# The tail of a decode block: a diagonal product moved forward, first-layer products interleaved, and the output stored after a block transpose on VectorE

## The chip, the cores and the metric

The kernel runs on one core of one Trainium2 chip. The metric is the device time of one execution in microseconds (us). The kernel before takes 667.69 us (median of 3 runs, 667.66 to 667.77). Nine executions of this kernel in one set of rounds lay between 667.60 and 667.92 us, so one kernel spreads by up to about 0.3 us, and its median moved from 667.69 to 667.81 us between sets of rounds.

Engine names as in the profile: PE is the matrix engine and PEld its weight loads, DVE is VectorE, ACT is ScalarE (the Activation engine), POOL is GpSimd, SP is the engine that issues DMAs. ACTq and SPq are the DMA issues of ACT and SP. A DMA has "landed" when the last increment of its completion semaphore has come. P.V is the product of the softmax weights with the values, oT its result for one quad (explained below), and yo the kernel's result before it is transposed and stored.

## The reference, cut to what matters

```python
x = A_x                                            # (4, 1, 512)
mod = (_silu(c) @ w_mod)...                        # six modulation vectors sa, ca, ga, sb, cb, gb
h = _layernorm(x) * (1 + ca) + sa
x = x + ga * attention(h, k_cache, v_cache, wq, wo)   # 4 batches, 32 heads, 4096 keys of 128: 268 MB of cache
h = _layernorm(x) * (1 + cb) + sb
z = gelu(h @ w_in)                                 # w_in: 512 x 1792
z1, z2 = z[..., :896], layernorm(z[..., 896:])
y = (z1 * (z2 * w_sp + b_sp)) @ w_out              # the sequence length is 1: w_sp and b_sp are scalars
return x + gb * y                                  # (4, 1, 512), bf16
```

The key and value caches stream through the core once. Everything else is small, but the last weights (wo, w_in, w_out) arrive at the end of the stream, and the feed-forward part can only follow them.

## The kernel before

The work goes over 32 "quads" (four heads of one batch element). The last quad (31) takes its P.V product in another form than the others, with v as weights, because v comes in five pieces:

```python
def values_last(i, n0, n1):
    P4 = P4s[i % NB]
    if n0 == 0:
        zsum(i)
    for n in range(n0, n1):
        nc.tensor.matmul(st["o", i], lhsT=st["v", i][:, n, :], rhs=P4[:, n, :], ...)
...
values_last(NQ - 1, 0, 3 * NT // 4)
diagonal(NQ - 2)                 # f32 products (four calls, eight in the trace) that take quad 30's result out of its block form
project(NQ - 2)                  # divide by the softmax sum into oT
values_last(NQ - 1, 3 * NT // 4, NT)
project(NQ - 1)                  # oT of quad 31, then the product with the last wo
```

After the attention, the first layer is 56 products from two w_in tiles (a=0: three quarters of the rows, a=1: the last quarter, loaded after it), first for z2 (s=1), then for z1 (s=0):

```python
for s in (1, 0):
    for a, (a0, a1) in enumerate(WJS):             # WJS = [(0, 3), (3, 4)]
        ...                                        # 21 products for a=0, 7 for a=1
            nc.tensor.matmul(zp[s][:, jf], lhsT=win[a][:, j - a0, cols], rhs=h[:, j], ...)
```

The result yo has the model dimension over the partitions. It is transposed on PE, copied from PSUM by DVE, and stored by one DMA of 16 rows of 256 bytes:

```python
nc.vector.tensor_tensor(out=yo.rearrange("p b j -> p j b"), in0=q, in1=r1, op=ALU.add)
t_ps = psum_s.tile([J * B, P], F32, name="small", bufs=1)
nc.tensor.matmul(t_ps, lhsT=yo.rearrange("p b j -> p (b j)"), rhs=ident, start=True, stop=True)
ot = post.tile([J * B, P], BF16, name="ot")
nc.vector.tensor_copy(out=ot, in_=t_ps)
nc.sync.dma_start(out=out.rearrange("b s (j p) -> (b s j) p", p=P), in_=ot)
```

## Time and profile before

| | before |
|---|---|
| time | 667.69 us |
| span of the profile | 666.0 us |
| mean rate of the loads | 425 GB/s |
| last wo lands, projection starts | 654.54, 654.58 us |
| yo ends | 662.89 us |
| store issued, landed | 663.60, 664.97 us |

The page of the profile first: its length, the mean busy share of the DMA engines in 40 slices (in tenths), and the first line of the chain that ended last.

```profile
span 666.0 us, 6938 instructions
...
DMA  9999999999999999999999999999999999999995
...
DMA 58%; PE 26%; DVE 14%; ACT 1%; issue 1%; SPq 0%; DVEq 0%; ACTq 0%
```

The loads are busy everywhere except in the last slice. The change touches the last 20 us only, so most of the time cannot move. The chain of waits from 630 us on (start, length, what):

```profile
631.71 22.83 DMA wo_g<-in_A_wo_dram
...
654.58 0.60 PE attn_ps L401 x16
...
658.24 0.77 PE z_ps L491 x21
...
659.05 1.25 PE z_ps L491 x35
...
660.56 1.28 ACT L506
...
663.26 0.28 DVE ot L535
```

The projection waits for the load of the last wo; then follow the statistics, the z products, the load of the activation table at 660.56, and the output. The timeline shows the instructions that the change moves (start, length, engine and line, operation, in brackets the idle time before and what ended it):

```profile
651.57 1.85 PE L354 MATMUL zo_ps<-sel,osb 128*128 128x4 f32 x8
...
653.28 0.99 PE L364 MATMUL zo_ps<-P_1_109,vt 128*128 128x4 bf16 x32
...
654.31 0.17 DVE L376 TENSOR_TENSOR oT<-zo_ps,rz 128x4 bf16<-128x4 f32 x1 [0.38 <-PE zo_ps L364]
654.58 0.51 PEld L401 LDWEIGHTS <-wo_g 128*128 128x128 bf16 x16 [0.39 <-DMA wo_g<-in_A_wo_dram]
...
658.21 0.72 PEld L491 LDWEIGHTS <-win_434 128*128 128x128 bf16 x21 [1.86 <-DMA win_434<-in_B_w_in_dram]
...
659.04 0.29 PEld L491 LDWEIGHTS <-win_435 128*128 128x128 bf16 x7
...
659.26 0.72 PEld L491 LDWEIGHTS <-win_434 128*128 128x128 bf16 x21
...
660.32 0.22 ACT L502 ACTIVATE u<-z_ps 128x56 bf16<-128x56 f32 x1 [0.67 <-PE z_ps L491]
...
662.70 0.20 DVE L529 TENSOR_TENSOR yo<-q,r_4229 128x16 bf16<-128x16 f32 x1
...
662.95 0.28 PE L531 MATMUL small<-ident,yo 128*16 128x128 bf16 x1 [1.24 <-DVE yo L529]
663.26 0.28 DVE L535 CAST ot<-small 16x128 bf16<-16x128 f32 x1 [0.37 <-PE small L531]
663.60 0.36 SPq L536 DMA_DIRECT2D out_dram<-ot  x1
```

Three things are to be seen. The diagonal stands at 651.57, between two pieces of the last P.V. The projection at 654.58 had a DMA as its last releaser, not oT. From the end of yo to the issue of the store 0.71 us pass.

Last, what SP waited for in the same view, from 662 us on:

```profile
SPq L562 <- DMA out_dram<-ot: 0.8, 1, 0.8
```

That is the end of the program: SP waits for the store to land.

### The profile page before, as it was taken

The numbers are of one execution on the slowest core, as the hardware profiler recorded it, in microseconds if no ns is written. First come the engines' busy times: TensorE is split into PE (matmuls) and PEld (weight loads), VectorE is DVE, ScalarE is ACT, GpSimd is POOL, SyncE is SP. The second block draws the span as 40 slices with busy tenths as digits, with TensorE's granted clock in tenths as the row PEclk, the third lists the DMA queues.
The fourth block names the chain that finished last, engine by engine and source line by source line (L and its number), as shares of the span: only waits on it lengthen the run. The fifth ranks groups of instructions, "written<-read, shape, count | busy, mean of one in ns | idle before, by whom it ended". The sixth has DMA issues, their size and how long they took to land.

```text
span 666.0 us, 6938 instructions
## 1 busy us (share of the span) xinstructions
PE 413.0 (62%) x3024; PEld 203.9 (31%) x3024; DVE 402.8 (60%) x475; ACT 41.3 (6%) x115; POOL 4.7 (1%) x21
## 2 busy tenths in 40 slices
PE   2567777646577664576655577655566656557765
PEld 2223333322233322232222333222223322223335
DVE  2166677665556575547576456757555757655762
ACT  1200000000000000000000000000000000000002
POOL 2000000000000000000000000000000000000000
PEclk9977777768887677887676787766788757788895
DMA  9999999999999999999999999999999999999995
GB/s 378 432 428 431 434 433 430 432 435 430 431 434 435 430 428 436 435 426 432 439 433 422 434 441 430 423 437 439 428 433 429 439 429 434 429 436 431 430 415 226
DMA packets 12733, 283.17 MB, mean 425 GB/s; under 512 B 1432, under 2 KB 1952, under 8 KB 4000
## 3 DMA queue, kind: packets, MB, share of 16 engines
q1 hardware_dynamic: 12624, 282.73, 98.8%
q8 instruction: 23, 0.38, 0.2%
q14 instruction: 6, 0.05, 0.0%
q0 software_dynamic: 64, 0.00, 0.0%
q10 hardware_dynamic: 16, 0.01, 0.0%
HBM read 282.73 MB, written 0.00 MB: 425 GB/s over the span
## 4 chain that ended last, share of the span: by engine, by line
DMA 58%; PE 26%; DVE 14%; ACT 1%; issue 1%; SPq 0%; DVEq 0%; ACTq 0%
DMA kt<-in_A_k_cache_dram 55%; PE s_ps L281 25%; DVE kt L276 12%; DMA wo_g<-in_A_wo_dram 3%; DVE S L290 0%; SPq L92 0%; PE z_ps L491 0%; PE big L341 0%; ACT E L311 0%; DVE P_0_105 L314 0%; ACT L506 0%; DVE nm L308 0%; DVE mT L300 0%; DVE hm L302 0%; DVE hb L304 0%
## 5 line engine op out<-in xcount | busy, mean ns | idle before, releaser
L281 PE MATMUL s_ps<-kt,ident 128*128 128x512 bf16 x1024 | 291.9, 455 | 188.1 <-DVE kt L276 188.1
L276 DVE TENSOR_TENSOR kt<-kt,qbc 128x8192 bf16<-128x8192 bf16 x64 | 282.7, 4420 | 84.2 <-DMA kt<-in_A_k_cache_dram 84.1
L281 PEld LDWEIGHTS <-ident 128*128 128x128 bf16 x1024 | 115.8, 113 | 352.9 <-issue 228.3
L290 DVE TENSOR_REDUCE S<-s_ps 128x64 f32<-128x512 f32 x64 | 44.3, 692 | 123.9 <-PE s_ps L281 123.9
L354 PE MATMUL zo_ps<-sel,osb 128*128 128x4 f32 x248 | 33.9, 260 | 25.8 <-ACT osb L347 25.8
L311 ACT ACTIVATE E<-S,nm 128x128 f32<-128x128 f32 x32 | 12.8, 402 | 566.1 <-DVE nm L308 566.1
L354 PEld LDWEIGHTS zo_ps<-sel,osb 128*128 128x128 f32 x248 | 31.4, 198 | 37.2 <-ACT osb L347 37.2
L341 PE MATMUL big<-vt,P_0_105 128*32 128x512 bf16 x352 | 21.0, 380 | 1.5 <-DMA vt<-in_A_v_cache_dram 1.5
L341 PE MATMUL big<-vt,P_1_109 128*32 128x512 bf16 x320 | 19.1, 380 | 0.0
L341 PE MATMUL big<-vt,P_2_113 128*32 128x512 bf16 x320 | 19.1, 380 | 0.0
L347 ACT COPY osb<-big 128x512 f32<-128x512 f32 x31 | 17.6, 566 | 18.3 <-PE big L341 18.3
L314 DVE TENSOR_TENSOR P_1_109<-E,mask_99 128x512 bf16<-128x512 f32 x11 | 7.6, 693 | 6.8 <-ACT E L311 6.8
L314 DVE TENSOR_TENSOR P_0_105<-E,mask_99 128x512 bf16<-128x512 f32 x11 | 7.6, 693 | 6.7 <-ACT E L311 6.7
L215 PE MATMUL big<-vt,hbc 128*32 128x512 bf16 x128 | 8.6, 434 | 5.0 <-DMA vt<-in_A_wq_dram 5.0
L341 PEld LDWEIGHTS <-P_0_105 128*32 128x32 bf16 x352 | 8.4, 96 | 8.9 <-DMA vt<-in_A_v_cache_dram 1.6
L314 DVE TENSOR_TENSOR P_2_113<-E,mask_99 128x512 bf16<-128x512 f32 x10 | 6.9, 692 | 6.2 <-ACT E L311 6.2
L375 DVE RECIPROCAL rz<-zo_ps 128x4 f32<-128x4 f32 x31 | 5.5, 176 | 8.2 <-PE zo_ps L354 8.2
L401 PE MATMUL attn_ps<-oP,wo_g 128*128 128x4 bf16 x112 | 3.8, 164 | 10.6 <-DVE oP L398 10.6
L341 PEld LDWEIGHTS <-P_2_113 128*32 128x32 bf16 x320 | 7.6, 96 | 6.7
L341 PEld LDWEIGHTS <-P_1_109 128*32 128x32 bf16 x320 | 7.6, 96 | 6.7
L401 PEld LDWEIGHTS <-wo_g 128*128 128x128 bf16 x128 | 4.3, 97 | 10.9 <-issue 10.4
L308 DVE STREAM_TRANSPOSE nm<-hb 128x32 f32<-128x32 f32 x32 | 6.8, 212 | 1.1
(218 smaller groups left out, 130.3 us busy)
## 6 DMA issues: line engine op xcount, KB each, us to landing
kt<-in_A_k_cache_dram SPq DMA_DIRECT2D x31, 4096.0 KB, 25.7
vt<-in_A_v_cache_dram SPq DMA_DIRECT2D x31, 4096.0 KB, 33.7
vt<-in_A_wq_dram SPq DMA_DIRECT2D x1, 4096.0 KB, 20.5
wo_g<-in_A_wo_dram SPq DMA_DIRECT2D x8, 512.0 KB, 26.6
kt<-in_A_k_cache_dram SPq DMA_DIRECT2D x2, 2048.0 KB, 24.1
vt<-in_w_mod_dram SPq DMA_DIRECT2D x1, 3072.0 KB, 10.0
vt<-in_A_v_cache_dram SPq DMA_DIRECT2D x1, 2048.0 KB, 18.8
win_434<-in_B_w_in_dram SPq DMA_DIRECT2D x1, 1344.0 KB, 24.3
```

Of the source, the lines that this page charges most:

```text
L215: nc.tensor.matmul(qp[hl * R:(hl + 1) * R, 0:n], lhsT=hbc[:, j, b, :], rhs=wv[:, g0:g0 + n, hl, :], start=(j == 0), stop=(j == J - 1), til ...
L276: nc.vector.tensor_tensor(out=kt, in0=kt, in1=q[:, None, :].to_broadcast([P, HT, DH]), op=ALU.mult,)
L281: nc.tensor.matmul(ps, lhsT=ident, rhs=kt[:, :, cc * DC:(cc + 1) * DC], start=(cc == 0), stop=(cc == DH // DC - 1),)
L290: nc.vector.tensor_reduce(out=st["S", i][:, half * HT:(half + 1) * HT], in_=st.pop(("s", i, half)), axis=AX.X, op=ALU.add,)
L308: nc.vector.transpose(out=nm, in_=hb)
L311: nc.scalar.activation(out=E, in_=S, func=AF.Exp, bias=nm[:, 0:1], scale=att_scale, accum_out=rs,)
L314: nc.vector.tensor_tensor(out=P4[:, 0:NT, :], in0=E[:, :, None].to_broadcast([P, NT, NH]), in1=mask4[:, None, :].to_broadcast([P, NT, NH]) ...
L341: nc.tensor.matmul(po[32 * t:32 * t + 32], lhsT=P4[:, n0:n0 + 8, :], rhs=st["v", i][:, n0:n0 + 4, :], start=(u == 0), stop=(u == NU - 1), ...
L347: nc.scalar.copy(out=osb, in_=po)
L354: nc.tensor.matmul(st["o", i], lhsT=osb[:, n, :], rhs=sel[:, NH * n:NH * n + NH], start=(n == 0), stop=(n == 3),)
L375: nc.vector.reciprocal(out=rz, in_=st.pop(("z", i)))
L401: nc.tensor.matmul(attn_ps[:, jo, :], lhsT=wo_g[:, hl, jo * P:(jo + 1) * P], rhs=oT[:, hl, :], start=(g == 0 and hl == 0 and jo == 0), sto ...
```

## The change

The intent: move the diagonal of quad 30 into time in which PE waits for v, so that the last P.V is not held up; give PE nine z1 products to do where z2 would wait for the second w_in tile; and shorten the output by transposing 32x32 blocks on DVE, straight into SBUF. The block transpose puts 16 useful rows at the head of each 32 partitions, so four stores are needed, two on SP and two on ACT. The core of the diff:

```diff
-        values_last(NQ - 1, 0, 3 * NT // 4)
         diagonal(NQ - 2)
         project(NQ - 2)
-        values_last(NQ - 1, 3 * NT // 4, NT)
+        values_last(NQ - 1)
         project(NQ - 1)
 ...
+        yo = post.tile([P, 2, B, J], BF16, name="yo")
+        nc.gpsimd.memset(yo, 0.0)
 ...
-        for s in (1, 0):
-            for a, (a0, a1) in enumerate(WJS):
-            ...                                   # products in the order of the loops
+        z0a = zmm[0, 0]
+        for s, jf, a, j in zmm[1, 0] + z0a[:9] + zmm[1, 1] + z0a[9:] + zmm[0, 1]:
+            ...                                   # the same 56 products
 ...
-        t_ps = psum_s.tile([J * B, P], F32, name="small", bufs=1)
-        nc.tensor.matmul(
-            t_ps, lhsT=yo.rearrange("p b j -> p (b j)"), rhs=ident, start=True, stop=True,
-        )
-        ot = post.tile([J * B, P], BF16, name="ot")
-        nc.vector.tensor_copy(out=ot, in_=t_ps)
-        nc.sync.dma_start(out=out.rearrange("b s (j p) -> (b s j) p", p=P), in_=ot)
+        ot = post.tile([P, R], BF16, name="ot")
+        nc.vector.transpose(out=ot, in_=yo.rearrange("p t b j -> p (t b j)"))
+        ov = out.rearrange("b s (j k r) -> k (b s j) r", j=J, r=R)
+        for k in range(P // R):
+            eng = nc.sync if k % 2 == 0 else nc.scalar
+            eng.dma_start(out=ov[k], in_=ot[k * R:k * R + B * J])
```

I call the three pieces part 1 (diagonal), part 2 (z1 products) and part 3 (output).

More of the change, by code (lines that the diff above doesn't have):

```diff
@@ L357, in diagonal, with values_last @@
                 )
-        def values_last(i, n0, n1):
+        def values_last(i):
             P4 = P4s[i % NB]
-            if n0 == 0:
-                zsum(i)
-            for n in range(n0, n1):
+            zsum(i)
+            for n in range(NT):
                 nc.tensor.matmul(
@@ L483 @@
         zp = {s: psum.tile([P, JF, B], F32, name=f"z{s}_ps") for s in (1, 0)}
+        zmm = {}
         for s in (1, 0):
             for a, (a0, a1) in enumerate(WJS):
-                for j0, j1 in JFS:
-                    for jf in range(j0, j1):
-                        c0 = s * FH + j0 * P + jf - j0
-                        cols = slice(c0, c0 + (P - 1) * (j1 - j0) + 1, j1 - j0)
-                        for j in range(a0, a1):
-                            nc.tensor.matmul(
-                                zp[s][:, jf], lhsT=win[a][:, j - a0, cols], rhs=h[:, j],
-                                start=(j == 0 and jf == 0), stop=(j == J - 1),
-                                skip_group_check=True,
-                            )
+                zmm[s, a] = [
+                    (s, jf, a, j) for jf in range(JF) for j in range(a0, a1)
+                ]
+        z0a = zmm[0, 0]
+        for s, jf, a, j in zmm[1, 0] + z0a[:9] + zmm[1, 1] + z0a[9:] + zmm[0, 1]:
+            j0, j1 = JFS[jf >= JFS[0][1]]
+            c0 = s * FH + j0 * P + jf - j0
+            nc.tensor.matmul(
+                zp[s][:, jf],
+                lhsT=win[a][:, j - WJS[a][0], c0:c0 + (P - 1) * (j1 - j0) + 1:j1 - j0],
+                rhs=h[:, j], start=(j == 0 and jf == 0), stop=(j == J - 1),
+                skip_group_check=True,
+            )
         z2b = post.tile([P, 2, JF, B], F32, name="z2b")
@@ L527 @@
         nc.vector.tensor_tensor(out=q, in0=q, in1=bc(rstd, J), op=ALU.mult)
-        yo = post.tile([P, B, J], BF16, name="yo")
-        nc.vector.tensor_tensor(out=yo.rearrange("p b j -> p j b"), in0=q, in1=r1, op=ALU.add)
-        t_ps = psum_s.tile([J * B, P], F32, name="small", bufs=1)
-        nc.tensor.matmul(
-            t_ps, lhsT=yo.rearrange("p b j -> p (b j)"), rhs=ident, start=True, stop=True,
-        )
-        ot = post.tile([J * B, P], BF16, name="ot")
-        nc.vector.tensor_copy(out=ot, in_=t_ps)
-        nc.sync.dma_start(out=out.rearrange("b s (j p) -> (b s j) p", p=P), in_=ot)
+        nc.vector.tensor_tensor(
+            out=yo[:, 0].rearrange("p b j -> p j b"), in0=q, in1=r1, op=ALU.add,
+        )
+        ot = post.tile([P, R], BF16, name="ot")
[4 more added lines that the diff above has]
+            eng.dma_start(out=ov[k], in_=ot[k * R:k * R + B * J])
 _INS = ['A_x', 'A_k_cache', 'A_v_cache', 'A_wq', 'A_wo', 'B_x', 'B_w_in', 'B_w_sp', 'B_b_sp', 'B_w_out', 'c', 'w_mod']
```

## The prediction

> **What bounds the kernel now.** The page shows the DMA engines at 9 tenths or more in 39 of 40 slices, 425 GB/s over a span of 666.0 us. The change touches only what comes after 645 us, so almost none of the 667.69 us can move. In the chain of waits the tail runs: load of the last wo_g lands at 654.54 -> projection 654.58 -> h ends 658.09 -> z products 658.24 to 660.28 -> gelu u 660.32-660.54 -> table load to 661.84 -> Ln, Exp to 662.39 -> q -> yo ends 662.90 -> PE transpose to 663.24 -> cast to 663.54 -> store issued 663.60, landing 1.4 us later -> end 666.0.
>
> **Part 1, diagonal 30 and project(30) ahead of the last P.V.** The timeline shows the eight f32 products (1.85 us) at 651.57-653.42 between the P.V pieces. PE is idle 645.7-648.27 and osb is copied by 646.01, so they move into idle time. The last P.V can then follow the last v piece (landing about 653.1), and the last oT end near 653.7 instead of 654.48. But the projection then waits for wo_g, landing at 654.54: before it began at 654.58, with a DMA as the last releaser. Gain at most 0.1 us, estimated 0.03.
>
> **Part 2, z1 products where z2 waits for w_in.** This trace has no such wait: the z2 products of the first w_in tile end at 659.02, those of the second start at 659.05. All 56 products remain, so gelu u still comes at about 660.3. The nine products put first (about 37 ns each) delay gelu z2 by about 0.33 us, from 659.46 to about 659.8, still ahead of gelu u. The z2 statistics product moves from 660.14 to about 660.26, y's start from 660.81 by at most 0.1, mostly hidden by the table load, which bounds rstd. Effect 0 to +0.1 us.
>
> **Part 3, output.** Removed after yo: a PE product (0.28), a cast from PSUM (0.28) and hops, 0.64 us in all. Added: one DVE block transpose; the kernel's own 128x32 ones take 0.21 us, so ot is ready about 0.24 us after yo: 0.40 us earlier. (The Trainium skill, "VectorE: DVE Perf Modes", The three transpose paths: on VectorE only 32x32 blocks, into SBUF. Hence four stores.) But each queue now issues two stores. SP issues take 0.33-0.43 us here, the out store 0.36; the Activation queue's two at the start took 0.56 and 0.26. The second issue thus starts about 0.35-0.6 us after the first, near 663.6-663.8, like the old single store. The Trainium skill ("DMA: Bandwidth & Descriptors", Issuing engines are not separate DMA queues) says a second issuer saves only issue time. Sum: -0.1 to +0.2 us.
>
> **Sum.** Part 1 -0.03, part 2 +0.02, part 3 -0.1 (estimates): 667.58 us, range 667.1 to 668.1. Chances: faster by over 2% 0.01, within 2% 0.98, slower 0.01.
>
> **What would show it.** Diagonal 30 at about 646-648 and the last oT before 654, yet the projection still released by wo_g near 654.5. Gelu z2 near 659.8, gelu u within 0.1 of 660.3 after the same landing. The DVE transpose 0.2 us, the first store issued about 0.3 us after yo (was 0.70), the second about 0.4 after that, landing 1.4 us after its issue.
>
> **What would make it wrong.** wo_g landing earlier than the trace suggests (then part 1 pays up to 0.7 us); stores of 64 bytes landing slower than those of 256; a slow first issue on the Activation queue; w_in landing later (then part 2 pays up to 0.3 us).

## More of the kernel before

Weight loads that do not wait overlap in this trace: the 7 of win_435 begin at 659.04 and take 0.29, yet the next group begins at 659.26. But the first group ends at 658.93 and win_435 begins only at 659.04. There is a gap of 0.11 us, which no bracket reports.

## The result, and the profile after

The changed kernel takes 668.17 us (median of 6 runs, 668.05 to 668.27), the kernel before 667.72 us in the same rounds (6 runs, 667.66 to 667.93). Ratios are the mean time of one kernel's runs over that of the other's of the same rounds, so not quite the ratio of the medians: 1.0006 with an interval of 0.9993 to 1.0019. By that interval the two are the same. In microseconds the two sets of six runs do not overlap, and by their medians the change costs 0.45 us. The prediction said 667.58 us with a range of 667.1 to 668.1. The measured time lies 0.07 us above the range, and the sign of the small difference was wrong.

The same views of the changed kernel. The page:

```profile
span 666.2 us, 6941 instructions
...
DMA  9999999999999999999999999999999999999995
...
DMA 61%; PE 24%; DVE 12%; ACT 1%; issue 0%; SPq 0%; DVEq 0%
```

The chain of waits:

```profile
632.45 22.09 DMA wo_g<-in_A_wo_dram
...
654.58 0.60 PE attn_ps L400 x16
...
658.24 1.87 PE z_ps L494 x56
...
660.37 1.28 ACT L510
...
662.74 0.21 DVE ot L537
```

The timeline:

```profile
646.07 1.06 PE L354 MATMUL zo_ps<-sel,osb 128*128 128x4 f32 x8 [0.75 <-ACT osb L347]
...
653.68 0.17 DVE L375 TENSOR_TENSOR oT<-zo_ps,rz 128x4 bf16<-128x4 f32 x1 [6.05 <-PE zo_ps L363]
654.57 0.51 PEld L400 LDWEIGHTS <-wo_g 128*128 128x128 bf16 x16 [1.02 <-DMA wo_g<-in_A_wo_dram]
...
658.21 1.02 PEld L494 LDWEIGHTS <-win_434 128*128 128x128 bf16 x30 [1.86 <-DMA win_434<-in_B_w_in_dram]
...
659.15 0.30 PEld L494 LDWEIGHTS <-win_435 128*128 128x128 bf16 x7
...
660.13 0.22 ACT L506 ACTIVATE u<-z_ps 128x56 bf16<-128x56 f32 x1 [0.37 <-PE z_ps L494]
...
662.51 0.20 DVE L533 TENSOR_TENSOR yo<-q,r_4231 128x16 bf16<-128x16 f32 x1
662.74 0.21 DVE L537 STREAM_TRANSPOSE ot<-yo 128x32 bf16<-128x32 bf16 x1
662.99 0.85 ACTq L541 DMA_DIRECT2D out_dram<-ot  x2
663.02 0.83 SPq L541 DMA_DIRECT2D out_dram<-ot  x2
```

And SP's wait at the end:

```profile
SPq L567 <- DMA out_dram<-ot: 1.1, 1, 1.1
```

The diagonal moved into idle time and the last oT comes 0.63 us earlier (653.68 for 654.31), but the projection starts at the same 654.58, released by wo_g. The 56 z products are one unbroken run (the win_435 group begins before the end of the group ahead of it), and gelu u comes 0.19 us earlier at 660.13 for 660.32. The transposed output is ready 0.59 us earlier. And still the span is longer. The chain now ends at 662.95, and what follows is not in it.

To see the end, I read from the trace when each store's semaphore increments came and what SP did afterwards. SP ends the program by waiting for the semaphores that the program's DMAs and engines use, one or two in each wait, one wait after the other. "Landed" is the last of a store's 16 increments; SP's "closing drain" is its first instruction after all these waits that signals the other engines. Times in us from the start of the span:

| | before | after | difference |
|---|---|---|---|
| projection starts | 654.58 | 654.58 | -0.01 |
| yo ends | 662.89 | 662.71 | -0.19 |
| last store issued | 663.60 | 663.43 | -0.18 |
| last store landed | 664.97 | 664.98 | +0.01 |
| SP's closing drain | 665.23 | 665.42 | +0.18 |
| span | 665.98 | 666.17 | +0.19 |
| time of this run | 667.75 | 668.05 | +0.30 |

So in these two executions 0.19 us were gained before the output, 0.20 lost up to the last landing, 0.17 lost between the landing and SP's drain, and 0.11 lost outside the span. The profiled execution of the changed kernel is the fastest of its six, which is why its difference is 0.30 and that of the medians 0.45. (Differences are taken before rounding.) The waits of SP, as the trace has them (start and length; before, the store's semaphore is the fourth waited for, after, the last store's is the second):

```
before   664.016 0.028   wait 1
         664.080 0.028   wait 2
         664.142 0.028   wait 3
         664.990 0.028   wait 4: the store (landed 664.974)
         665.052 0.028   wait 5
         665.111 0.028   wait 6
         665.179 0.007   wait 7
         665.234 0.007   closing drain
after    663.902 0.017   wait 1
         663.955 1.051   wait 2: the last store (landed 664.984)
         665.046 0.028   wait 3
         665.110 0.028   wait 4
         665.172 0.028   wait 5: first store on ACT (landed 664.351)
         665.231 0.028   wait 6: first store on SP (landed 664.518)
         665.293 0.028   wait 7: second store on ACT (landed 664.821)
         665.358 0.007   wait 8
         665.416 0.007   closing drain
```

A wait whose semaphore is long complete still costs about 0.06 us. Those ahead of the landing are free; those behind it are not.

### The profile page after: what moved, and what is told of

It is laid out like the page before. It is cut to its first block, busy times and chain, and to the rows that moved or that the text cites. A ratio compares the mean times of both kernels' runs of the same rounds, so it can differ in the third digit from the quotient of the medians.

```text
span 666.2 us, 6941 instructions
## 1 busy us (share of the span) xinstructions
PE 414.6 (62%) x3022; PEld 203.6 (31%) x3023; DVE 402.8 (60%) x475; ACT 41.3 (6%) x115; POOL 4.8 (1%) x22
## 4 chain that ended last, share of the span: by engine, by line
DMA 61%; PE 24%; DVE 12%; ACT 1%; issue 0%; SPq 0%; DVEq 0%
DMA kt<-in_A_k_cache_dram 58%; PE s_ps L281 24%; DVE kt L276 11%; DMA wo_g<-in_A_wo_dram 3%; SPq L92 0%; PE z_ps L494 0%; PE big L341 0%; DVE S L290 0%; ACT L510 0%; ACT E L311 0%; DVE P_1_109 L314 0%; DVE P_0_105 L314 0%; PE small L155 0%; PE attn_ps L400 0%; DVE mT L300 0%
## 5 line engine op out<-in xcount | busy, mean ns | idle before, releaser
L354 PEld LDWEIGHTS zo_ps<-sel,osb 128*128 128x128 f32 x248 | 30.0, 191 | 38.4 <-ACT osb L347 38.4
L375 DVE TENSOR_TENSOR oT<-zo_ps,rz 128x4 bf16<-128x4 f32 x32 | 5.4, 169 | 7.1 <-PE zo_ps L363 6.0
```

The costliest lines, as they stand in the source:

```text
L354: nc.tensor.matmul(st["o", i], lhsT=osb[:, n, :], rhs=sel[:, NH * n:NH * n + NH], start=(n == 0), stop=(n == 3),)
L375: nc.vector.tensor_tensor(out=oT[:, :, b], in0=st.pop(("o", i)), in1=rz, op=ALU.mult,)
```

## The experiments

My theory: parts 1 and 2 gain a little; part 3 loses it and more, (a) because the second store of each queue is issued 0.4 us after the first, (b) because two stores issued at once complete one after the other, (c) because the last store's semaphore is among the first that SP waits for, and (d) by something after the span. Rivals: the reordering of PE hurts; stores of 64-byte rows are slow by themselves; the second queue is slow. "Against before" compares medians of the same rounds.

### Part 1 alone

```diff
-        values_last(NQ - 1, 0, 3 * NT // 4)
         diagonal(NQ - 2)
         project(NQ - 2)
-        values_last(NQ - 1, 3 * NT // 4, NT)
+        values_last(NQ - 1)
```

> Part 1 alone (diagonal 30 and project(30) ahead of the last P.V; z order and output as before). Both theories: the last oT ends near 653.8 us but the projection still starts at 654.58 us because wo_g lands then, so the time equals the kernel before within 0.08 us. If part 1 were the cause of the loss, +0.3 us or more.

Measured: 667.68 us (667.53 to 667.88) against 667.81 us (667.60 to 667.92), -0.13 us, a little more than the 0.08 that I allowed and with ranges that overlap. The projection started at 654.58 us, 0.05 after wo_g landed at 654.53. Part 1 is not the loss.

### Parts 1 and 2, with the old output

Taken from the changed kernel, with the output of before put back:

```diff
-        yo = post.tile([P, 2, B, J], BF16, name="yo")
-        nc.gpsimd.memset(yo, 0.0)
 ...
-        ot = post.tile([P, R], BF16, name="ot")
-        ...                                # block transpose, four stores
+        ...                                # PE transpose, copy, one store, as before
```

> Parts 1 and 2 with the old output (PE transpose, cast, one store of 16 rows of 256 bytes). My theory: the changed z order removes a hidden wait of about 0.17 us for the second w_in tile, so 0.15 to 0.22 us faster than before, and the whole loss sits in the output. Rival (the reordering hurts): slower than before by 0.2 us or more.

Measured: 667.67 us (667.58 to 667.70) against 667.81, -0.14 us: at the edge of what I expected, and the rival fails. In the total it cannot be told from part 1 alone, because wo_g happened to land 0.10 us later in this profile (654.63). From the first z product to the end of yo it takes 4.47 us, as in the changed kernel (4.47); the three runs with the old z order took 4.65 (before), 4.57 (part 1 alone) and 4.54 (part 3 alone, below). So part 2 is worth 0.07 to 0.18 us, and its worth depends on how long after h the second w_in tile lands. The z products themselves show it without exception: from the first start to the last they take 1.69 us here and in the changed kernel, 1.88, 1.80 and 1.77 us in the three with the old order. (In three later runs with part 2, yo came 4.52 to 4.63 us after the first z product although the z products took no longer; in the run with the unused tile the trace shows y waiting for the last w_out tile.) In the kernel before, the second w_in tile landed at 659.00 and the first product with it started at 659.05, 0.195 us after the one ahead of it; with part 2 no two z products start more than 0.05 us apart.

### Part 3 alone

```diff
+        yo = post.tile([P, 2, B, J], BF16, name="yo")
+        nc.gpsimd.memset(yo, 0.0)
 ...
-        ...                                # PE transpose, copy, one store
+        ...                                # block transpose, four stores, as in the change
```

> Part 3 alone on the kernel before. My theory: the last store lands about 0.2 us later after yo than the old one, SP then has about 0.18 us more of semaphore checks, and something after the span adds about 0.1: +0.45 to +0.7 us against before. Rival (the loss comes from parts 1 and 2): within 0.15 us of before.

Measured: 668.28 us (668.12 to 668.44) against 667.81, +0.47 us. The whole loss is in part 3. The last store landed 2.28 us after yo (before: 2.08), SP's drain came 0.43 us after the landing (before: 0.26), and 1.95 us of the profiled time lay outside the span (before: 1.77): 0.20 + 0.17 + 0.18 us. Part 1's absence shows too: here the projection started at 654.64, released by oT, 0.13 us after wo_g landed, so part 1 is worth up to 0.08 us in some executions.

```profile
654.64 0.57 PE L401 MATMUL attn_ps<-oT,wo_g 128*128 128x4 bf16 x16 [0.26 <-DVE oT L376]
```

### The order of the last waits

The loads of c and x are cut, which changes which semaphore each later DMA uses. The last store's semaphore is then waited for fifth of the eight (I had written "fourth of seven"; what matters is what follows it).

```diff
-    nc.scalar.dma_start(out=rows[0:B], in_=c)
-    nc.scalar.dma_start(out=rows[B:2 * B], in_=A_x.rearrange("b s d -> (b s) d"))
+    xr = A_x.rearrange("b s d -> (b s) d")
+    for src, r0, cuts in ((c, 0, [0, 1, 2, 3, 4]), (xr, B, [0, 1, 2, 4])):
+        for a, b in zip(cuts[:-1], cuts[1:]):
+            nc.scalar.dma_start(out=rows[r0 + a:r0 + b], in_=src[a:b])
```

> The changed kernel with the loads of c and x at the start cut into 7 instead of 2, which moves every later DMA by five completion semaphores, so that the last store's semaphore is the fourth of the seven that SP checks at the end, as the old store's was, not the second. My theory: 0.10 to 0.15 us faster than the changed kernel (about +0.3 us against before instead of +0.45). Rival (the number or the size of the stores alone costs the time): the same as the changed kernel, +0.45 us against before.

Measured: 667.85 us (667.81 to 668.02) against 667.81, +0.04 us, so about 0.4 us better than the changed kernel was in its own rounds, more than I expected. The wait did what the theory says: from the last landing to the drain 0.261 us, as before, instead of 0.432. The step outside the span is gone as well (1.77 us instead of 1.88), which I had not counted on. These make 0.17 + 0.11 = 0.28 us. The rest is mostly the yardstick: the kernel before measured 667.81 us in these rounds and 667.72 us in those of the changed kernel, and without it the two medians (667.85, 668.17) differ by 0.32 us. Cutting loads at the start also moves the start of the stream, so this kernel is not a clean change of one thing.

### One store, two stores, four stores on one queue

These ask what a store costs. The first two store only a quarter and a half of the output. Their outputs are wrong, which doesn't matter for the times.

```diff
-        for k in range(P // R):
+        for k in range(1):
```

> The changed kernel with only the first of its four stores (16 rows of 64 bytes, on SP), so three quarters of the output are wrong on purpose. My theory (rows of 64 bytes cost nothing, the count of stores does): the store lands about 1.37 us after its issue, as the 256-byte rows did, so about 1.68 us after yo instead of 2.07 to 2.08, and the time is about 0.5 us below the kernel before. Rival (64-byte rows land slower): landing 1.5 us or more after the issue.

```diff
-        for k in range(P // R):
+        for k in range(2):
```

> The changed kernel with the first two of its four stores, one on each queue, so half of the output is wrong on purpose. My theory: both are issued at once, but their completions come one after the other, so the later lands about 1.50 us after its issue, 0.13 later than in one_block; time within 0.0 to 0.2 us of one_block. Rival (the two queues are independent): both land about 1.37 us after their issue.

```diff
-            eng = nc.sync if k % 2 == 0 else nc.scalar
+            eng = nc.sync
```

> The changed kernel with all four stores on the SP queue. My theory: each further issue costs about 0.42 us on the queue, so the last is issued about 1.25 us after the first and lands about 0.7 us later than in the changed kernel: +1.0 to +1.3 us against before. Rival (completions, not issues, set the pace, or the second queue is what hurts): at or below the changed kernel's +0.45 us.

The issues in the three timelines, first one block, then two, then four on SP:

```profile
662.67 0.21 DVE L537 STREAM_TRANSPOSE ot<-yo 128x32 bf16<-128x32 bf16 x1
662.94 0.36 SPq L541 DMA_DIRECT2D out_dram<-ot  x1
```

```profile
662.48 0.21 DVE L537 STREAM_TRANSPOSE ot<-yo 128x32 bf16<-128x32 bf16 x1
662.73 0.38 ACTq L541 DMA_DIRECT2D out_dram<-ot  x1
662.76 0.36 SPq L541 DMA_DIRECT2D out_dram<-ot  x1
```

```profile
662.80 0.21 DVE L537 STREAM_TRANSPOSE ot<-yo 128x32 bf16<-128x32 bf16 x1
663.07 1.75 SPq L541 DMA_DIRECT2D out_dram<-ot  x4
```

The landings, from the trace (us from a store's issue to its last increment, in order of issue):

| kernel | rows | each store | last landing after yo |
|---|---|---|---|
| before | 256 B | 1.37 | 2.08 |
| one block | 64 B | 1.35 | 1.66 |
| two blocks, ACT and SP | 64 B | 1.37, 1.50 | 1.81 |
| changed kernel, ACT, SP, ACT, SP | 64 B | 1.37, 1.50, 1.42, 1.56 | 2.28 |
| four on SP | 64 B | 1.35, 1.39, 1.40, 1.40 | 3.04 |

Times: one block 667.20 us (667.06 to 667.32), two blocks 667.59 us (667.34 to 667.73), four on SP 668.76 us (668.72 to 668.91), each against 667.70 us. One block is 0.50 us below the kernel before, as expected: the short path works, and rows of 64 bytes cost nothing against rows of 256. Two stores at once do not finish at once: the 16 increments of the ACT store came from 663.924 to 664.096, those of the SP store from 664.102 to 664.262. They follow each other about 10 ns apart, one store after the other, and the second lands 0.15 us later than alone. It is the second to complete that is late, not the queue: in the run with the unused tile (below) SP's first store completed first, in 1.35 us, and that of ACT second, in 1.55 us. On one queue each further issue costs 0.41 to 0.46 us, and the later stores land only 0.04 to 0.05 us later after their issue, with their increments well apart. Four on SP are +1.06 us, as expected, so the second queue does help: the rival that it hurts falls. Only the total of two blocks misses: 0.39 us above one block, where I had allowed 0.2. Its span is 0.09 us shorter than one block's (its wo_g landed 0.13 us earlier), but 2.12 us of its profiled time lay outside the span, against 1.78.

### The step after the span

> The changed kernel with five one-element activations and their table load at the start on the Activation engine, nothing else. It asks what the 0.10 to 0.14 us after the last traced instruction are, which the changed kernel and the one with the output alone showed and the one with the moved semaphores did not. If it is where the Activation engine's instruction stream ends: that step is gone and the time is about +0.3 us against before. If it is the semaphores or the second queue: still there, +0.45 us.

```diff
+    pad = persist.tile([1, 8], F32, name="pad")
+    for i in range(5):
+        ...                                # memset of pad[:, i:i + 1] on the Activation engine
```

Measured: 671.82 us (671.70 to 672.05) against 667.70, +4.12 us, which no theory had. The step itself was gone: 1.77 us outside the span, and the drain still 0.432 us after the landing. But the loads were slower from the beginning, so the total answers nothing. The small tile had been allocated ahead of all load targets. So I put the activations elsewhere, and tried the tile without them:

```diff
+        pad = pre.tile([P, B], F32, name="pad")        # the last tile of the start-up pool
+        for _ in range(5):
+            nc.scalar.activation(out=pad, in_=rstd, func=AF.Exp)
```

> The changed kernel with five small activations into a scratch tile of the start-up phase (which moves no later tile). If the step of 0.10 to 0.14 us after the last traced instruction depends on where the Activation engine's instruction stream ends, it is gone and the time is +0.3 to +0.35 us against before; otherwise +0.45 us. The landing to SP's drain stays at 0.43 us in both cases.

```diff
+    pad = persist.tile([1, 8], F32, name="pad")        # 32 bytes per partition, allocated first
+    nc.gpsimd.memset(pad, 0.0)
```

> The changed kernel with one unused tile of 32 bytes per partition allocated first, written once on POOL. It asks where the 3.6 us of the run with the activations at the start came from. If from the addresses of the load targets, which the tile moved by 32 bytes: again about 3.6 us slower than the changed kernel, growing evenly over the whole run. If from the activations or the table load: the same as the changed kernel, +0.45 us against before.

Measured: with the activations in the start-up pool 668.04 us (667.93 to 668.10) against 667.74, +0.30 us; 1.81 us outside the span, the drain still 0.433 us after the landing, as expected. With the tile alone 671.93 us (671.58 to 672.02) against 667.74, +4.19 us. So the activations take the step away, and the tile makes the slowdown, about 3.7 us (4.19 less the 0.45 of the changed kernel). Of the pages, the changed kernel and then the one with the tile:

```profile
span 666.2 us, 6941 instructions
...
DMA packets 12829, 283.17 MB, mean 425 GB/s; under 512 B 1528, under 2 KB 2048, under 8 KB 4096
```

```profile
span 669.7 us, 6942 instructions
...
DMA packets 12829, 283.17 MB, mean 423 GB/s; under 512 B 1528, under 2 KB 2048, under 8 KB 4096
```

The packets are the same in number and size, but the rate falls from 425 to 423 GB/s. A packet of 32 KB took 1219.3 ns on average, for 1214.5, and the loss grows evenly: the last q times k product started at 633.69 us in the changed kernel and at 636.80 with the tile. After the first microseconds, all that the tile does by its edit is to move the addresses of later tiles by 32 bytes. The traces hold no addresses and no other shift was tried, so that the addresses are the cause is argued by elimination.

What the step is stays argued. After the last traced instruction the trace shows a series of final increments of one semaphore. In the changed kernel the last but one comes 0.131 us after its forerunner, with part 3 alone 0.145 us, with the unused tile 0.131 us, in the kernel before and in both kernels with more activations 0.034 to 0.035 us. Kernels with five or more further instructions on ACT also show one more fetch of 8 KB of instructions on one of the two instruction queues, at 667.59 us in the run with the activations in the start-up pool. That fits an instruction fetch which falls into the last few instructions, but no run shows the engine waiting for it.

### The two outputs with the best order of waits

```diff
+    for src, r0, cuts in ((c, 0, [0, 2, 4]), (xr, B, [0, 2, 4])):   # parts 1 and 2, old output
 ...
+    for a in range(B): ...                 # the changed kernel: c in 4 rows, x in 3 rows and 2 halves
```

> Parts 1 and 2 with the old output, and the loads of c and x cut in two each, so that the one store uses the semaphore that SP checks last. My theory: the end of the landing to SP's drain falls from 0.26 to 0.14 us, so 0.20 to 0.30 us faster than the kernel before and the best of all that compute the right result. Rival (the order of the checks does not matter): -0.10 us, like parts 1 and 2 alone.

> The changed kernel with the loads of c and x cut into 9, so that its last store uses the semaphore that SP checks last. My theory: from the last landing to SP's drain 0.14 us instead of 0.43 us; the time about -0.1 to +0.05 us against before, still 0.15 to 0.25 us above the version with the old output, as its last store lands 0.2 us later after yo. Rival: +0.3 us or more.

Measured: 667.80 us (667.71 to 668.14) and 668.44 us (667.94 to 669.00), against 667.74. Both miss. The waits behave as the theory says: 0.139 and 0.140 us from the landing to the drain. For parts 1 and 2 the span shrank to 665.62 us, 0.27 below that of parts 1 and 2 without the cut loads (about 0.12 of it from the waits, 0.16 because the projection started at 654.52 instead of 654.68), but 2.09 us of the time lay outside the span instead of 1.79. That gives it back, as with two blocks; what goes with it stands under "What stays open". For the changed kernel nine small loads at the start disturbed the stream. SP waited 6.9 us for the semaphore of a piece of c before it could issue the load of wq, at 8.07 us (1.17 in the kernel before), and the projection started at 655.83 us instead of 654.58. A gain at the end that is bought with a change at the start is not reliable here.

The best right version measured is therefore parts 1 and 2 with the old output: 667.67 us, 0.14 below before and, over different rounds, about 0.5 below the changed kernel. Part 1 alone, at 667.68 us, is as good within the noise. The interval of the former against before (0.9984 to 1.0012) does not exclude that it is equal.

## Why the prediction was right or wrong

Two steps failed. The one that made the forecast wrong is the sum of part 3: it was put at -0.1 us and measured +0.47 us, because it ended at the landing of the last store, took that landing 0.16 us too short, and left out everything that comes after it.

**Part 1: right.** Diagonal 30 moved to 646.07, oT came at 653.68, the projection stayed at 654.58. The last wo sets the pace, and 0.63 us of gain became wait.

**Part 2: wrong step.** The prediction said "This trace has no such wait", read from matmuls that "end at 659.02" and a next start at 659.05. Those ends are not observed. The Trainium skill ("Perfetto Trace Analysis", Tensor Engine Instruction) says that the profiler estimates the end of a TensorE instruction. One product is shown with 0.17 us while the next starts 0.03 us after it. The start-to-start gap of 0.195 us at the change of the tile was the wait. Its worth, 0.07 to 0.18 us, was put down as a cost of 0.02. Two of the signs named for it failed with it: gelu z2 came at 659.58, not near 659.8, and gelu u at 660.13, not within 0.1 us of 660.3. It was luck that this error ran against that of part 3 and hid some of the loss.

**Part 3: one term was too small, and two were missing.** The prediction had "Sum: -0.1 to +0.2 us" and put -0.1, the low end, into the total; part 3 alone measured +0.47 us. The transpose was right: 0.21 us and ot 0.25 us after yo. So was the second issue, about 0.4 us after the first. So the last issue came 0.72 us after yo, where the old single one came 0.71 us after it: the shorter transpose was used up, as the prediction's own text says ("like the old single store"). But "landing 1.4 us after its issue" was 1.56 us for the last store, where one alone took 1.35. About 0.15 us of the difference comes from two stores that finish together and take turns in completing, about 0.05 us from being the second on its queue. The Trainium skill ("DMA: Bandwidth & Descriptors", Why a DMA increments its semaphore by 16 and not by 1) says that every engine taking part posts one increment; the traces show 16 for each store, spread over 0.15 to 0.20 us, and those of two stores in sequence (in one run they overlap by 0.01 us). With a landing of 1.4 us the last store would have landed 2.12 us after yo, +0.04 us against before; it landed at 2.28, +0.20 us. The missing terms were SP's waits behind the landing (0.17 us) and the step after the span (0.11 to 0.18 us). The first is shown by the three runs that moved the wait. Of the second only its place and what removes it are shown.

**What would make it wrong.** Of the four named causes none came true as the reason: wo_g did not land earlier, 64-byte rows landed as fast as 256-byte rows, the first issue on ACT took 0.38 us, and the second w_in tile landed no later (658.96 for 659.00); its wait was there already and worked in favour of the change.

**What stays open.** The time outside the span belongs to the kernel: in all executions of one kernel it is the same to about 0.1 us. In the profiled runs it goes with the number of ACT's instructions in the trace:

| instructions of ACT | kernels | outside the span |
|---|---|---|
| 181 | before, part 1, parts 1 and 2, one block, four on SP | 1.77 to 1.80 |
| 183 | two blocks, parts 1 and 2 with cut loads | 2.12, 2.09 |
| 184 | changed kernel, part 3 alone, unused tile | 1.88 to 1.95 |
| 189, 190 | order of waits, both with activations | 1.77 to 1.81 |
| 191 | changed kernel with nine loads | 1.86 |

That suggests that both steps come from the length of ACT's instruction stream. It is a correlation over 14 kernels: only the five activations vary that length and little else, and they test the smaller step alone. The larger one, of 0.3 us, is not in the closing increments, whose last comes 1.91 and 1.94 us after the span's end, close to the kernels without a step (1.90 to 1.93). And the parts, measured apart (-0.14 and +0.47), add up to +0.33 us where the change measured +0.45 in its own rounds. That difference of 0.12 us is as large as the spread of single runs.

## What to carry to other kernels

Count a tail to the end of the program, not to the issue of the last store: the landing, the completions that take turns, and the waits behind the last landing are all in the time. Here, splitting one small store into four needed more than the 0.4 us that the shorter transpose saved, because each further issue on a queue cost 0.4 us. And read waits of PE from start-to-start distances, because the shown ends can close over a gap, as they did over the 0.195 us here.

## What the Trainium skill lacked or had wrong

- "DMA: Bandwidth & Descriptors", Issuing engines are not separate DMA queues: it says that a second issuer saves only the time of issuing, and the runs agree (four stores on one queue landed 3.04 us after yo, on two queues 2.28). It gives no time for how far the completions of two small stores issued at once lie apart: here 16 increments about 10 ns apart for each, the second store 0.15 us later.
- The same page, Specifications, sets 512 bytes as the least size for full rate. It has no landing time of one small store issued by SP or ACT by the size of its rows: 16 rows of 64 bytes landed in 1.35 us and 16 rows of 256 bytes in 1.37 us, both below that size.
- No page I read has the cost of the program's closing waits: about 0.06 us for each wait of SP that follows the last landing, 0.14 to 0.43 us in all by their order.
- "SBUF — State Buffer", Operand start alignment, says of its rule on start addresses that it is about legality, not speed. So it leaves the speed open. Here an edit that shifts the load targets by 32 bytes slowed a 32 KB packet from 1214.5 to 1219.3 ns and the whole run by about 3.7 us, more than anything that the change did; that it is the addresses is argued.
- "Runtime: NRT & Kernel Launch", Instruction fetch mechanics, calls the cost of a block boundary mostly hidden. The runs show a step of about 0.1 us after the last traced instruction (0.131 and 0.145 us between two increments, for 0.034) that five more activations on ACT take away. That it is a fetch is argued, not shown.
